# Two fused layers on one core: the last head pair's attention output is turned by a DMA transpose instead of TensorE

## The chip, the cores and the metric

The kernel runs on one core of one Trainium2 chip. The metric is the device time of one execution in microseconds (us). Engines are named as the profile names them: PE is TensorE (PEld its weight loads), DVE is VectorE, ACT is ScalarE, POOL is GpSimd, SP is SyncE, which here only issues DMAs.

## The reference, cut to what matters

Causal attention over 4 batches, 8 heads, 768 positions and head size 64, in which some heads see everything before them and the others only 4 sink positions and a window of 64. Its output, as 3072 tokens by 512, goes through a linear layer, a PReLU with one slope per column and a second linear layer:

```python
mask = np.where(retr[0, :, 0, 0, None, None], full_mask, stream_mask)
scores = np.where(mask[None, :, :, :], scores, -1000000000.0)
a = softmax(scores)                       # over the keys
attn_out = np.matmul(a, v)                # (4, 8, 768, 64)
x = attn_out.transpose(0, 2, 1, 3).reshape(B * S, H * D)
h = x @ w_in                              # 512 -> 2048
g = np.maximum(h, 0.0) + alpha * np.minimum(h, 0.0)
return (g @ w_out).astype(np.float32)     # 2048 -> 512
```

## The kernel before

The heads of a batch are taken two at a time, in the pairs (2, 6), (1, 5), (0, 4), (3, 7); with four batches that makes 16 pairs, numbered n = 0 to 15, so that pairs 12 to 15 are the last batch. Every piece of work is an item with a name, and the list `ORDER` gives the order in which all items are issued, written out by hand. Each engine runs its own share of that list in order; between engines, semaphores hold an instruction until its inputs are there. The items that matter here, with n a pair, h one of its two heads and m a part:

- `Sn.h.m` are the score matmuls (PE, L421 to L438), `sn.h.m` their exponentials on ACT (L477 for heads that see everything, L524 and L526 for windowed ones), and `mn.h.m` the masks, which DVE multiplies in (L486, and L535 with L538 for windowed heads).
- `An.h` is the product of the exponentials with the values on PE (L562), `an.h` the division by the row sums on DVE (a reciprocal, L572, and a product, L573) into a buffer `xn`.
- `Xn` turns `xn`, in which rows are tokens, into `xT`, in which columns are tokens. Pairs 0 to 3 do it in `X_pe`, with one transpose of TensorE per tile into a PSUM bank (L587), and `xn` with a small x (`x15` and the like, L592) copies the bank to `xT` on DVE. Later pairs do it in `X_dma` (L581), one DMA transpose from SP's queue. Pair 15 is the exception among the later ones: it takes `X_pe` and the copy `x15`.
- `Pt.f` is a block of the first linear layer for token block t (t = 0 to 7, two per batch: 512 tokens and 256). It takes one PSUM bank and adds up four terms, one for each pair of the batch, in the order of the pairs (L607); so it reads all four pairs' rows of `xT`, pair 15's last in batch 3. `pt.f` is the first half of the PReLU on ACT (L612), `gt.f` the second on DVE (L619).
- `Ot.s.u` is a quarter of an output piece of the second layer, four matmuls of 512 columns (L627); `ot.s` copies the finished piece out of its bank on ACT (L633) and writes it to memory (L637), from POOL's queue for t below 6 and from SP's above. `L0` to `L2` and `l0` to `l2` are the last piece, cut in three (L646, L655, L656).

Pair 15 is a pair of two windowed heads, with seven tiles of 112 queries each. A PSUM bank is taken by `take`, which picks the one given back longest ago, and is given back by `give`. So the order of the items also settles which bank each of them gets.

The buffer `xn` has three copies in use in turn; the fourth pair of a batch writes the copy that was used three pairs earlier and waits until the transfer that reads it is over.

In the last batch the items around the change are issued in this order: the products A12.1, A14.1 and A14.0, then six quarters of output pieces of blocks 4 and 5, then A15.0 and A15.1, two quarters, the seven transposes X15, one quarter, and then P6.11, the first block of the first layer for this batch. On SP's queue X13, X14 and X12 follow one another.

Of the kernel before, what the change touches and what calls it, by code (L numbers as in the profile page):

```python
# [63 lines left out]
m13.1.0 m14.0.0 m13.0.1 S14.0.5 S13.0.0 O4.2.2 O4.2.3 s13.1.2 m13.1.2 m13.1.1 s13.0.0 s14.0.4 s14.0.5 m13.0.2 S12.1.0 m12.1.5 s14.1.2 S12.1.3  # L64
S15.0.0 S14.0.3 m13.0.0 A13.1 o4.2 s12.1.0 s12.1.2 A13.0 s15.0.0 O5.0.0 s12.1.3 s14.0.3 m14.0.4 Cv15 a13.1 O5.0.1 a13.0 S15.0.1
S15.0.2 m12.1.0 S15.1.0 S15.1.2 S15.1.1 S14.0.2 O4.1.0 s15.0.2 s15.1.0 m12.1.4 s14.0.2 s15.1.1 m14.1.1 m14.0.5 m14.1.2 m12.1.3 m14.1.0 A12.1
m14.0.3 A14.1 A14.0 a14.0 s15.1.2 a14.1 m15.0.2 s15.0.1 a12.1 O4.1.1 X13 O4.0.0 O4.0.1 O4.0.2 O4.0.3 m15.0.0 m15.1.1 O4.1.2
m15.0.1 m15.1.2 m15.1.0 A15.0 o4.0 A15.1 a15.0 O4.1.3 a15.1 O5.0.2 X15 O5.0.3 X14 x15 o4.1 o5.0 X12 P6.11
p6.11 P6.2 P6.15 P6.10 p6.10 P7.4 P6.0 P6.1 g6.11 g6.10 p6.1 P6.6 P7.8 p6.15 g6.15 g6.1 p6.0 g6.0
P6.5 p7.4 p6.5 p6.6 g7.4 g6.6 g6.5 P6.3 P6.12 P7.2 p6.3 p6.12 g6.12 p6.2 g6.2 P6.4 p7.8 P7.6  # L70
P6.14 g6.3 g7.8 p7.6 p6.4 g7.6 g6.4 P7.10 P6.7 P6.8 p6.8 p6.7 P7.0 P6.9 P6.13 g6.7 p7.2 g7.2
g6.8 p7.10 g7.10 p6.9 P7.14 O6.3.0 P7.12 p6.13 g6.13 p7.12 O6.0.0 O6.0.1 O6.1.0 p7.0 g7.0 g6.9 O6.3.1 O7.0.0
O6.3.2 O6.1.1 p7.14 p6.14 g6.14 g7.12 O6.3.3 o6.3 O6.0.2 O6.1.2 O6.1.3 o6.1 O6.0.3 o6.0 O6.2.0 O6.2.1 O6.2.2 O7.0.1
O7.0.2 O6.2.3 o6.2 m12.0.2 g7.14 L2 l2 O7.0.3 o7.0 L0 L1 l1 warm1 l0
""".split()


# [1 line left out]
def kernel(  # L79
# [20 lines left out]
    bf16 = DT.bfloat16  # L100
# [4 lines left out]
    NT = 7  # L105
    SLOT = 288
    LAY = 4
# [24 lines left out]
    def tiles(n):  # L132
        return FULL if full(n) or mixed(n) else NEAR if n >= LAY else FAR
# [5 lines left out]
    NSEG = 4 * B  # L139
# [4 lines left out]
    work = ctx.enter_context(tc.tile_pool(name="work", bufs=2))  # L144
# [6 lines left out]
    def take(*choices):  # L151
        got = min((c for c in choices if all(age[b] >= 0 for b in c)), key=lambda c: max(age[b] for b in c))
        for b in got:
            age[b] = -1
        return got

    def give(got):
        for b in got:
            age[b] = stamp[0]
            stamp[0] += 1  # L160
# [3 lines left out]
    def bank(b):  # L164
        return P[:, b, :]

    def bank_bf(b):
        return P[:, b, :].bitcast(bf16)
# [34 lines left out]
    def heads(n):  # L203
        return PAIRS[n % 4]
# [89 lines left out]
    def item(name, fn, *args):  # L294
        I[name] = lambda: fn(*args)

    MISC = [(6,), (7,)]
    ANY = [(b,) for b in (0, 1, 2, 3, 4, 5, 6, 7)]
# [7 lines left out]
    natq, natk, held = {}, {}, {}  # L306
# [56 lines left out]
    def to_array(key, nat, choices, first_half=False):  # L363

        held[key] = take(*choices)
        tr = bank_bf(held[key][0])
        for i in range(6):
            if first_half:
                nc.tensor.transpose(tr[0:D, 128 * i:128 * (i + 1)], nat[:, i, 0:D], ident)
            else:  # L370
                nc.tensor.transpose(tr[:, 128 * i:128 * (i + 1)], nat[:, i, :], ident)
# [168 lines left out]
    xn = {}  # L540
# [24 lines left out]
    def AV_out(n, hh):  # L565
        got = held.pop(("A", n, hh))
        nt = len(tiles(n).QS)
        pav = bank(got[0])[:, 0:nt * (D + 1)].rearrange("p (i c) -> p i c", c=D + 1)
        if n not in xn:
            xn[n] = work.tile([128, NT, 128], bf16, tag="xn", name="xn", bufs=3)  # L570
        rcp = work.tile([128, NT, 1], fp32, tag=f"rcp{hh}", name="rcp")[:, 0:nt]
        nc.vector.reciprocal(rcp, pav[:, :, D:D + 1])  # L572
        nc.vector.tensor_tensor(xn[n][:, 0:nt, D * hh:D * hh + D], pav[:, :, 0:D],  # L573
                                rcp.to_broadcast([128, nt, D]), op=ALU.mult)
        give(got)
# [6 lines left out]
                          xn[n][0:r, 0:nt].rearrange("p i c -> p (i c)"), transpose=True)  # L582

    def X_pe(n):
        held["X", n] = got = take(*(MISC if n < 4 else ANY))
        for i, x in enumerate(tiles(n).QS):
            nc.tensor.transpose(bank_bf(got[0])[:, x:x + 128], xn[n][:, i, :], ident)  # L587

# [168 lines left out]
    for n in range(NSEG):  # L757
        if n:
            item(f"Lq{n}", load_q, n)
            item(f"Cq{n}", cast_q, n)  # L760
        item(f"Lk{n}", load_k, n)
        item(f"Lv{n}", load_v, n)
        if n == 3:
            for hh in range(2):
                item(f"Cv{n}.{hh}", cast_v_head, n, hh)
        else:
            item(f"Cv{n}", cast_v, n)
        if n < CROSS:
            for hh in range(2):
                item(f"Ck{n}.{hh}", cast_k, n, hh)  # L770
            if n:
                two = [(4,), (5,)] if n < 4 else ANY
                item(f"Tq{n}", lambda n=n, two=two: to_array(("q", n), natq[n], two))
                item(f"tq{n}", put_q, ("q", n), n, slice(0, 128), "A")
                item(f"Tk{n}", lambda n=n, two=two: to_array(("k", n), natk[n], two))
                for hh in range(2):
                    item(f"tk{n}.{hh}", put_k, ("k", n), n, hh, True)
        else:
            item(f"Ck{n}", cast_k_near, n)
            item(f"Dq{n}", dma_q, n)  # L780
            for hh in range(2):
                item(f"Dk{n}.{hh}", dma_k, n, hh)
        for hh, h in enumerate(heads(n)):
            k_ = (3 if n < 4 else 6) if RETR[h] else (2 if n < 4 else 3)
            for m in range(k_):
                item(f"S{n}.{hh}.{m}", S_retr if RETR[h] else S_stream, n, hh, m)
                item(f"s{n}.{hh}.{m}", E_retr if RETR[h] else E_stream, n, hh, m)
                if n >= 4:
                    item(f"m{n}.{hh}.{m}", M_retr if RETR[h] else M_stream, n, hh, m)
            item(f"A{n}.{hh}", AV, n, hh)  # L790
            item(f"a{n}.{hh}", AV_out, n, hh)
        if LAY <= n < NSEG - 1:
            item(f"X{n}", X_dma, n)
        else:
            item(f"X{n}", X_pe, n)
            item(f"x{n}", X_out, n)
# [61 lines left out]
```

## Time and profile before

| | |
|---|---|
| Median of 3 runs | 227.65 us (227.13 to 227.97) |
| Profiled execution, its own time | 227.53 us |
| Span of that execution in the profile | 225.8 us |
| PE busy | 221.3 us (98% of the span) |
| DVE busy, ACT busy, POOL busy | 148.4 (66%), 139.5 (62%), 45.2 (20%) us |
| PE's share of the chain that ended last | 70%; DMA 13%, SP's queue 11%, POOL 3% |
| Granted clock of TensorE | 1.0 |

The span is shorter than the execution's own time, by 1.7 us that lie around what the profiler sees. The chain that ended last is followed back from the last instruction: at each step to what released it. In the first 65 us it goes through loads and their issue on SP's queue, after that through PE. In a timeline a row gives the start in us, the length in us, the engine, the line, the operation and its operands; a bracket at its end tells how long the engine had been idle before it and what ended that. Matmuls are pipelined, so a single one looks longer in a timeline than the step from one to the next.

### The profile page before, as it was taken

How to read it: one execution, taken by the hardware profiler on the slowest of the kernel's cores; microseconds unless marked ns; L12 is line 12 of the kernel's file. 1: busy time of each engine (PE TensorE's matmuls, PEld its weight loads, DVE VectorE, ACT ScalarE, POOL GpSimd, SP SyncE). 2: the span in 40 equal slices, each digit the busy share in tenths (PEclk: the TensorE clock that was granted, in tenths of full speed). 3: DMA queues.
4: the chain of work that ended last, by engine and by line, in shares of the span. 5: the costliest groups of instructions: out<-in, count | busy, mean ns of one | idle time of the engine just before them, and what ended most of it. 6: DMA issues, size and time to landing. Idle time of an engine off the chain costs nothing.

```text
span 225.8 us, 5221 instructions
## 1 busy us (share of the span) xinstructions
PE 221.3 (98%) x1993; PEld 136.4 (60%) x1993; DVE 148.4 (66%) x396; ACT 139.5 (62%) x286; POOL 45.2 (20%) x91
## 2 busy tenths in 40 slices
PE   7999999999999999999999999999999999999994
PEld 7989876575555557564556455556556555664454
DVE  5799638995659618898798229977586526866000
ACT  3788668999888037577993147787584237563311
POOL 5689569400230001000401001000110100000000
DMA  6999999999999999999989999995822420000213
GB/s 200 310 242 207 266 214 273 212 196 218 198 245 222 140 245 190 197 190 186 236 194 153 237 231 205 188 164 108 124 94 40 115 96 0 0 4 0 93 71 116
DMA packets 95369, 37.38 MB, mean 166 GB/s; under 512 B 82392, under 2 KB 93552, under 8 KB 95344
## 3 DMA queue, kind: packets, MB, share of 16 engines
q1 hardware_dynamic: 89088, 27.72, 66.6%
q0 software_dynamic: 5792, 8.93, 17.1%
q10 hardware_dynamic: 464, 0.40, 0.5%
q8 instruction: 15, 0.25, 0.5%
q14 instruction: 10, 0.08, 0.1%
HBM read 27.71 MB, written 6.29 MB: 151 GB/s over the span
## 4 chain that ended last, share of the span: by engine, by line
PE 70%; DMA 13%; SPq 11%; POOL 3%; issue 1%; ACTq 0%; DVE 0%; POOLq 0%; DVEq 0%
PE P L627 31%; PE P L607 28%; DMA kf<-in_k_dram 8%; SPq L249 5%; PE P L562 5%; PE P L438 3%; DMA qf<-in_q_dram 3%; SPq L253 2%; DMA vf<-in_v_dram 2%; SPq L230 2%; PE P L646 2%; SPq L246 1%; POOL vb L356 1%; POOL g L322 1%; PE P L431 1%
## 5 line engine op out<-in xcount | busy, mean ns | idle before, releaser
L619 DVE SCALAR_TENSOR_TENSOR g<-neg,oma,P 128x256 bf16<-128x256 f32 (+1 forms) x128 | 71.0, 609 | 35.9 <-ACT neg L612 35.2
L607 PE MATMUL P<-xT,w_in_b 128*128 128x512 bf16 (+1 forms) x512 | 86.6, 326 | 0.0
L627 PE MATMUL P<-w_out_b,g 128*128 128x512 bf16 x368 | 85.3, 379 | 0.0
L612 ACT ACTIVATE neg<-P 128x512 f32<-128x512 f32 x96 | 54.2, 600 | 26.3 <-PE P L607 20.8
L607 PEld LDWEIGHTS <-w_in_b 128*128 128x128 bf16 x512 | 49.5, 98 | 32.3 <-DVE g L619 0.2
L627 PEld LDWEIGHTS <-g 128*128 128x128 bf16 x368 | 33.9, 98 | 37.2 <-issue 0.9
L477 ACT ACTIVATE eR<-P 128x448 bf16<-128x448 f32 (+3 forms) x63 | 35.9, 614 | 5.4 <-PE P L438 2.5
L633 ACT COPY ot<-P 128x512 f32<-128x512 f32 x23 | 13.8, 600 | 37.3 <-PE P L627 32.6
L637 POOL DMA_DIRECT2D out_dram<-ot x18 | 10.3, 574 | 108.9 <-ACT ot L633 108.7
L524 ACT ACTIVATE eS<-P 128x352 bf16<-128x352 f32 x45 | 20.4, 479 | 3.9 <-PE P L438 3.4
L573 DVE TENSOR_TENSOR xn<-P,rcp 128x448 bf16<-128x448 f32 (+1 forms) x32 | 19.0, 595 | 1.1
L535 DVE TENSOR_TENSOR eS<-eS,ms_near 128x352 bf16<-128x352 bf16 x45 | 14.4, 335 | 0.7 <-ACT eS L524 0.6
L572 DVE RECIPROCAL rcp<-P 128x7 f32<-128x7 f32 (+1 forms) x32 | 6.3, 197 | 11.2 <-PE P L562 10.5
L486 DVE TENSOR_TENSOR eR<-eR,mr_near 128x128 bf16<-128x128 bf16 x54 | 10.3, 219 | 3.9 <-ACT eR L477 3.7
L421 PE MATMUL P<-qT,kT 128*128 128x192 bf16 (+14 forms) x68 | 11.2, 251 | 0.2 <-DVE kT L394 0.2
L562 PEld LDWEIGHTS <-eS 128*128 128x128 bf16 x266 | 9.7, 97 | 2.3 <-issue 0.6
L562 PE MATMUL P<-vb,eS 128*128 128x65 bf16 x266 | 10.8, 193 | 0.0
L438 PEld LDWEIGHTS <-kT 64*128 64x128 bf16 x167 | 6.7, 94 | 6.1 <-issue 5.5
L438 PE MATMUL P<-qT,kT 64*128 64x176 bf16 (+7 forms) x167 | 10.3, 250 | 0.0
L562 PE MATMUL P<-vb,eR 128*128 128x65 bf16 x258 | 9.9, 193 | 0.1
L562 PEld LDWEIGHTS <-eR 128*128 128x128 bf16 x258 | 9.1, 97 | 1.4 <-issue 0.2
L655 DVE COPY ot<-P 128x128 f32<-128x128 f32 x1 | 0.3, 292 | 14.3 <-PE P L646 14.3
(96 smaller groups left out, 176.9 us busy)
## 6 DMA issues: line engine op xcount, KB each, us to landing
out_dram<-ot POOLq DMA_DIRECT2D x18, 256.0 KB, 3.9
kf<-in_k_dram SPq DMA_DIRECT2D x21, 192.0 KB
qf<-in_q_dram SPq DMA_DIRECT2D x18, 192.0 KB
vf<-in_v_dram SPq DMA_DIRECT2D x14, 196.0 KB
qf<-in_q_dram SPq DMA_DIRECT2D x7, 384.0 KB
vf<-in_v_dram SPq DMA_DIRECT2D x12, 192.0 KB
w_in_b<-in_moe_w_in_dram POOLq DMA_DIRECT2D x8, 256.0 KB, 9.1
w_out_b<-in_moe_w_out_dram POOLq DMA_DIRECT2D x4, 512.0 KB, 13.7
```

Of the source, the lines that this page charges most:

```text
L249: (nc.gpsimd if n == 13 and src is k else nc.sync).dma_start(dst[0:NSINK, :, hh, :], dram(src, o, [[D, NSINK], [0, NT], [1, D]]))
L438: nc.tensor.matmul(to, keys[own], queries[own], start=True, stop=True)
L477: nc.scalar.activation(ebuf[n, hh][:, lo:hi].rearrange("p (x c) -> p x c", x=len(parts)), P[:, got[0]:got[0] + len(parts), 0:(hi - lo) // ...
L524: nc.scalar.activation(slots, sc[:, 0:352].rearrange("p (s c) -> p s c", c=176), AF.Exp, scale=scale)
L535: nc.vector.tensor_tensor(slots, slots, ms_near[:, 0:2, :] if m == 0 else ms_near[:, 1:3, :], op=ALU.mult)
L562: nc.tensor.matmul(pav[:, i, :], e[:, o:o + 128], vv[:, j, hh, 0:D + 1], start=(m == 0), stop=(m == len(terms) - 1))
L573: nc.vector.tensor_tensor(xn[n][:, 0:nt, D * hh:D * hh + D], pav[:, :, 0:D], rcp.to_broadcast([128, nt, D]), op=ALU.mult)
L607: nc.tensor.matmul(psg[:, w * i:w * (i + 1)], w_in_b[:, c, 128 * fb:128 * (fb + 1)], xT[:, c, o:o + w], start=(x == 0), stop=(x == 3))
L612: nc.scalar.activation(neg[t, f], bank(held["P", t, f][0]), AF.Relu, scale=-1.0)
L619: nc.vector.scalar_tensor_tensor(g_buf[t % 2][:, fb, 0:w], neg[t, f][:, c], oma[:, fb:fb + 1], bank(got[0])[:, c], op0=ALU.mult, op1=ALU.add)
L627: nc.tensor.matmul(bank(held["O", t, s][0]), g_buf[t % 2][:, f, 128 * s:128 * (s + 1)], w_out_b[:, f, :], start=(f == 0), stop=(f == 15))
L633: nc.scalar.copy(ot, bank(got[0]))
```

## The change

Pair 15's output is turned by `X_dma`, one more DMA transpose on SP's queue, in place of seven transposes on PE and the copy on DVE. In the order, the masks of pair 15 move up in front of the divisions a14 and a12.1, and the products A15.0 and A15.1 move up in front of eight output quarters that had stood partly before, partly after them. The output quarters keep their order; X14 and X12 are issued among them and X15 behind the last of block 4. The buffer `xn` gets four copies. The exception in `X_pe` for late pairs, which no pair uses any longer, goes. What stands before and after the three lines of `ORDER` below is the same (the lines behind are only broken differently).

```diff
 ORDER
-m14.0.3 A14.1 A14.0 a14.0 s15.1.2 a14.1 m15.0.2 s15.0.1 a12.1 O4.1.1 X13 O4.0.0 O4.0.1 O4.0.2 O4.0.3 m15.0.0 m15.1.1 O4.1.2
-m15.0.1 m15.1.2 m15.1.0 A15.0 o4.0 A15.1 a15.0 O4.1.3 a15.1 O5.0.2 X15 O5.0.3 X14 x15 o4.1 o5.0 X12 P6.11
+m14.0.3 A14.1 A14.0 s15.1.2 m15.0.0 m15.0.2 m15.1.0 s15.0.1 m15.1.1 O4.1.1 X13 m15.1.2 m15.0.1 a14.0 a14.1 A15.0 A15.1 a12.1
+O4.0.0 X14 O4.0.1 O4.0.2 O4.0.3 X12 o4.0 a15.0 O4.1.2 a15.1 O4.1.3 X15 o4.1 O5.0.2 O5.0.3 o5.0 P6.11
...
     def AV_out(n, hh):
...
-            xn[n] = work.tile([128, NT, 128], bf16, tag="xn", name="xn", bufs=3)
+            xn[n] = work.tile([128, NT, 128], bf16, tag="xn", name="xn", bufs=4)
...
     def X_pe(n):
-        held["X", n] = got = take(*(MISC if n < 4 else ANY))
+        held["X", n] = got = take(*MISC)
...
-        if LAY <= n < NSEG - 1:
+        if n >= LAY:
             item(f"X{n}", X_dma, n)
         else:
             item(f"X{n}", X_pe, n)
             item(f"x{n}", X_out, n)
```

More of the change, by code (lines that the diff above doesn't have):

```diff
@@ L66 @@
 S15.0.2 m12.1.0 S15.1.0 S15.1.2 S15.1.1 S14.0.2 O4.1.0 s15.0.2 s15.1.0 m12.1.4 s14.0.2 s15.1.1 m14.1.1 m14.0.5 m14.1.2 m12.1.3 m14.1.0 A12.1
-m14.0.3 A14.1 A14.0 a14.0 s15.1.2 a14.1 m15.0.2 s15.0.1 a12.1 O4.1.1 X13 O4.0.0 O4.0.1 O4.0.2 O4.0.3 m15.0.0 m15.1.1 O4.1.2
-m15.0.1 m15.1.2 m15.1.0 A15.0 o4.0 A15.1 a15.0 O4.1.3 a15.1 O5.0.2 X15 O5.0.3 X14 x15 o4.1 o5.0 X12 P6.11
[L69 to L74, printed above, removed]
+m14.0.3 A14.1 A14.0 s15.1.2 m15.0.0 m15.0.2 m15.1.0 s15.0.1 m15.1.1 O4.1.1 X13 m15.1.2 m15.0.1 a14.0 a14.1 A15.0 A15.1 a12.1
+O4.0.0 X14 O4.0.1 O4.0.2 O4.0.3 X12 o4.0 a15.0 O4.1.2 a15.1 O4.1.3 X15 o4.1 O5.0.2 O5.0.3 o5.0 P6.11 p6.11
+P6.2 P6.15 P6.10 p6.10 P7.4 P6.0 P6.1 g6.11 g6.10 p6.1 P6.6 P7.8 p6.15 g6.15 g6.1 p6.0 g6.0 P6.5
+p7.4 p6.5 p6.6 g7.4 g6.6 g6.5 P6.3 P6.12 P7.2 p6.3 p6.12 g6.12 p6.2 g6.2 P6.4 p7.8 P7.6 P6.14
+g6.3 g7.8 p7.6 p6.4 g7.6 g6.4 P7.10 P6.7 P6.8 p6.8 p6.7 P7.0 P6.9 P6.13 g6.7 p7.2 g7.2 g6.8
+p7.10 g7.10 p6.9 P7.14 O6.3.0 P7.12 p6.13 g6.13 p7.12 O6.0.0 O6.0.1 O6.1.0 p7.0 g7.0 g6.9 O6.3.1 O7.0.0 O6.3.2
+O6.1.1 p7.14 p6.14 g6.14 g7.12 O6.3.3 o6.3 O6.0.2 O6.1.2 O6.1.3 o6.1 O6.0.3 o6.0 O6.2.0 O6.2.1 O6.2.2 O7.0.1 O7.0.2
+O6.2.3 o6.2 m12.0.2 g7.14 L2 l2 O7.0.3 o7.0 L0 L1 l1 warm1 l0
 """.split()
```

## The prediction

> **What bounds the kernel now.** I read the page's busy table first, then the chain that ended last in the stretch which the change touches, then the DVE, ACT and SP timelines there, and last the DMA shares by stage. TensorE (PE) is busy for 98% of the span:
>
> ```profile
> PE 221.3 (98%) x1993; PEld 136.4 (60%) x1993; DVE 148.4 (66%) x396; ACT 139.5 (62%) x286; POOL 45.2 (20%) x91
> ```
>
> The chain of waits from 170 to 186 us (start, length, what) runs on PE alone, with no step on another engine:
>
> ```profile
> 170.41 1.73 PE P L562 x57
> 172.14 5.18 PE P L627 x24
> 177.32 0.79 PE P L562 x26
> 178.11 1.73 PE P L627 x8
> 179.83 0.39 PE P L587 x7
> 180.22 0.86 PE P L627 x4
> 181.09 4.97 PE P L607 x27
> ```
>
> The reader sees in it the order of the code: A12.1, A14.1, A14.0 (L562), six output pieces of four matmuls (L627), A15.0 and A15.1, two pieces, the seven transposes X15 (L587), one piece, and then P6.11 (L607). PE never waits here, so an instruction that is taken off PE is worth its own time, and everything else is worth something only if it makes PE wait. From 181.09 to 222.70 the chain stays on PE (L607, L627, L646); the start of that block carries over to the end one to one.
>
> **The change part by part.** (1) Seven transposes leave PE: the chain gives 0.39 us for them, 56 ns each; the four matmuls after them take 0.86 us and the eight before 1.73, 0.216 each, so the switch costs nothing besides. Worth -0.39 us, and this is on the path. (2) The copy x15 (L592, 0.56 us) leaves DVE. DVE starts it at 180.26 and its next work, a prelu at 182.62, waits for ACT: worth nothing. (3) The masks m15 and the products A15 move up. What their masks need is this, in the DVE and the ACT timeline:
>
> ```profile
> 169.89 0.22 DVE L486 TENSOR_TENSOR eR<-eR,mr_near 128x128 bf16<-128x128 bf16 x1
> 172.25 0.20 DVE L572 RECIPROCAL rcp<-P 128x6 f32<-128x6 f32 x1 [2.13 <-PE P L562]
> ...
> 174.71 1.09 DVE L535 TENSOR_TENSOR eS<-eS,ms_near 128x352 bf16<-128x352 bf16 x4
> 175.72 0.20 DVE L538 TENSOR_TENSOR eS<-eS,ms_near 128x96 bf16<-128x96 bf16 x1
> 175.84 0.33 DVE L535 TENSOR_TENSOR eS<-eS,ms_near 128x352 bf16<-128x352 bf16 x1
> ```
>
> ```profile
> 171.24 0.31 ACT L526 ACTIVATE eS<-P 128x96 bf16<-128x96 f32 x1
> 171.37 0.53 ACT L524 ACTIVATE eS<-P 128x352 bf16<-128x352 f32 x1
> ```
>
> DVE is idle for 2.13 us after m14.0.3, waiting for A14.0. All eight mask instructions of pair 15 now stand in that hole: six of 0.26 us and two of 0.12 (steps from start to start) are 1.8 us of work. The first five can run from 170.02 on as their exponentials come; m15.1.2 needs the ACT instruction that ends at 171.55, and the last, m15.0.1, the one that ends at 171.90. So m15.0.1 runs from 171.94 to 172.28, and the reciprocal of a14.0 starts at about 172.25, where it starts now. Cost on DVE: nothing, hidden by the 2.13 us; without that cover it would be the 1.8 us, given on to a14, a12 and the transfers. On PE, A15.0 now comes after one output piece: 172.14 + 0.86 = 173.00. Its weight load that needs the last mask comes at about 172.9, so that mask has 0.6 us to spare. If it were later than that, PE and all that is queued on it would wait, one to one.
>
> (4) On DVE then a14.0, a14.1, a12.1 (0.70 us apart as now) end by 174.44, and a15.0, a15.1 (0.78 each, as in the rows from 177.75 to 179.38 now) by 175.98: A15.1 has ended on PE at 173.00 + 0.79 = 173.79, so they don't wait for it. The wait that a15.0 had for the landing of X13 goes with the fourth buffer; it had been over long before (X13's packets end at 171.0) and costs nothing now, so its loss is worth nothing. (5) One transfer is added on SP's queue, X15, behind X13, X14 and X12. X14 goes at 173.76 and X12 at 175.06 as now, because SP is held by X14 until 174.97 in both. X12 holds SP for 1.24 us, so X15 starts on SP at 176.36. Behind it on SP are only the outputs of blocks 6 and 7, from 201 on: nobody waits for that. The output writes of blocks 4 and 5 go through POOL; o4.0 now comes after PE's 173.79 + 3.46 = 177.25 and its write moves past X15's packets.
>
> When must X15 have landed? PE goes from 173.79 through 32 output matmuls, 32 x 0.216 = 6.91, to 180.70. P6.11 starts there, and its fourth matmul, the one that reads pair 15's rows of xT, is at 180.70 + 3 x 0.216 = 181.35. That is 5.0 us after X15 started on SP. The page gives no landing time for these transposes, so I bound it. From above by X7, the same pair's transfer two batches earlier (seven tiles of 112 rows too), in the SP timeline and the chain of that stage:
>
> ```profile
> 77.72 1.22 SPq L581 DMA_TRANSPOSE xT<-xn  x1
> ```
>
> ```profile
> 74.55 6.04 PE P L627 x28
> 80.60 17.34 PE P L607 x108
> ```
>
> There, too, the fourth matmul of the first block reads it, at 80.60 + 0.65 = 81.25, and PE did not wait: it landed within 3.53 us, while loads of later pairs shared the DMA engines. From below by X13 (seven tiles of 112 rows like X15), started on SP at 168.46; in the DMA shares (last two columns: share of the engines, GB/s) its packets are these:
>
> ```profile
> 169.60:170.00 0.40, 0.40 (x3) 0.19 (x2) 0.40 (x3) 0.40 (x3) 0.00 (x0) 1.00 0.78 152
> 170.00:170.40 0.40, 0.40 (x7) 0.24 (x6) 0.11 (x1) 0.40 (x2) 0.00 (x0) 1.00 1.10 208
> 170.40:170.80 0.40, 0.40 (x20) 0.40 (x17) 0.00 (x0) 0.40 (x2) 0.00 (x0) 1.00 0.70 142
> ```
>
> They end 2.4 us after the start. Between 2.4 and 3.5 us, X15 lands between 178.8 and 179.9 and has 1.5 to 2.5 us to spare. I take the upper end; both ends cost nothing. It is a close cover and not a wide one: 1.5 us later than X7's bound and PE begins to wait.
>
> The Trainium skill (VectorE: DVE Perf Modes, "The three transpose paths" and "Rules for kernel authors") speaks against this change: it gives 390 ns for one 128x128 turn on TensorE and 1309 ns by DMA, and advises TensorE where the result may go to PSUM. By its price the seven turns would be 2.73 us of PE; the trace has 0.39 us for all seven, queued back to back, and the trace decides.
>
> (6) P6 and P7 take other banks. The list of takes and gives is the same with the bank numbers exchanged, and each bank is given back before its next block needs it (the latest, o5.0's, serves P6.6, seven blocks on). Worth nothing.
>
> Sum against the profiled execution: span 225.80 - 0.39 = 225.41, and with the 1.73 us that lie around it (227.53 - 225.80) 227.14. That execution is 0.12 below the median of the three runs; on the median the forecast is 227.65 - 0.39 = 227.26.
>
> **The rivals.** *X15 lands late (slower).* Mechanism: the seven tiles are turned one after another, each as slow as a whole issue on SP, 1.22 us. Then it lands at 176.36 + 8.54 = 184.90 and PE waits 3.55 us in front of P6.11's fourth matmul: +3.16, 230.8. It begins to cost when the landing takes over 5.0 us, and gives a slower kernel by over 1.14 us (0.5%) from 6.5 us on. Against it: X7's 3.53 us and X13's packets, both of seven tiles. Taken one after another, the Trainium skill's 1309 ns a tile (VectorE: DVE Perf Modes, "The three transpose paths") would lead to the same wait; no row here bears it out. Chance 0.04; a smaller wait that leaves the kernel within 0.5% gets 0.05, with a time up to 228.4.
>
> *The masks become the bound.* If m15.0.1 comes as late as it does now, 176.17, A15.0 waits 3.3 us: +2.9, 230.5. It decides from 172.9 on. For it: DVE runs in order, and one late exponential holds everything behind it. Against it: the last exponential is there at 171.90 and ACT's order does not change. Chance 0.01.
>
> *The gain is larger.* If the fourth buffer took away waits of DVE in other batches that PE pays for, or if the interruption of the output pieces cost more than its 0.39 us, the kernel would gain over 1.14 us, say 226.2. The waits of the matmul queue list none after 66 us, so there is hardly anything to take. Chance 0.02.
>
> *Nothing changes:* the 0.39 us are lost again at P6's start, 227.65. Possible if DVE set the pace of block 6 from its first prelu; but it waits for ACT there, 1.80 us before the first one. Chance 0.08; this leaves 0.80 for the forecast.
>
> **How the numbers follow.** 0.5% (1.14 us) is about what a measurement of this kernel can tell from no change. Faster by more: 0.02. Slower by more: 0.04 + 0.01 = 0.05. Within it: 0.93, from the forecast, the small wait and no change. The range takes the forecast with the scatter of the three runs (0.52 below and 0.32 above their median), and no change with a little of a wait: 226.75 to 227.85.
>
> **What would show it.** Right: no L587 after 170 us; A15.0 at about 173.0 with no idle time before it; 32 matmuls of L627 in one piece for 6.9 us; the last transpose starts on SP near 176.4; P6.11 at 180.7 and the span near 225.4. Wrong: idle time of PE in front of L607 at 181 (X15 late) or of L562 at 173 (masks late), a reciprocal of a14.0 well after 172.3, or a stretch after P6.11 that has become longer than 41.6 us.

## The result and the profile after

The changed kernel took 227.1 us (median of 22 runs), the kernel before, run beside it, 228.11 us (22 runs); disturbed runs are left out of the ratio, which is 0.9953 with a 95% interval of 0.9933 to 0.9973. The forecast was 227.26 us and 0.9983. The profiled execution of the changed kernel took 226.85 us with a span of 225.1 us, 0.7 less than the 225.8 before; the steps of the trace account for 0.39 + 0.18 of it, and 0.11 stood there before the change begins.

PE's busy share is unchanged within what missing matmul records leave open (1958 records for 1986 weight loads here). The weight loads are seven fewer than before (1993), one for each transpose, and DVE has one instruction less, the copy:

```profile
PE 219.3 (97%) x1958; PEld 136.0 (60%) x1986; DVE 148.0 (66%) x395; ACT 139.5 (62%) x286; POOL 45.3 (20%) x91
```

The chain of waits in the stretch of the change, to be laid beside that of before:

```profile
170.30 1.73 PE P L562 x57
172.03 0.05 issue
172.08 0.81 PE P L627 x3
172.89 0.79 PE P L562 x26
173.68 4.32 PE P L627 x20
177.99 0.05 issue
178.05 2.54 PE P L627 x11
180.58 1.51 PE P L607 x7
```

A12.1, A14.1, A14.0, one output quarter, A15.0 and A15.1 directly behind it, then eight output quarters in one piece and P6.11. L587 is gone. An "issue" of 0.05 us with one matmul too few behind it (3 for 4, 20 and 11 for 32) is a matmul whose record is missing: the times go on without a gap. From the first L562 to the first L607 it was 181.09 - 170.41 = 10.68 us and is 180.58 - 170.30 = 10.28 us: 0.40 less. In PE's timeline, on which the table below rests, the two matmuls start at these times, first before, then after (10.67 and 10.28 us apart):

```profile
170.25 0.80 PE L562 MATMUL P<-vb,eR 128*128 128x65 bf16 x21
180.92 1.24 PE L607 MATMUL P<-xT,w_in_b 128*128 128x512 bf16 x5
```

```profile
170.14 0.80 PE L562 MATMUL P<-vb,eR 128*128 128x65 bf16 x21
180.42 1.89 PE L607 MATMUL P<-xT,w_in_b 128*128 128x512 bf16 x8
```

What follows P6.11 has not changed: from its start to the last copy on DVE (L655) 41.69 us before (181.09 to 222.78) and 41.70 after (180.58 to 222.28).

DVE's timeline shows the masks in the hole that was 2.13 us of idle time before:

```profile
169.78 0.22 DVE L486 TENSOR_TENSOR eR<-eR,mr_near 128x128 bf16<-128x128 bf16 x1
169.92 0.59 DVE L535 TENSOR_TENSOR eS<-eS,ms_near 128x352 bf16<-128x352 bf16 x2
...
171.83 0.34 DVE L535 TENSOR_TENSOR eS<-eS,ms_near 128x352 bf16<-128x352 bf16 x1
172.09 0.19 DVE L572 RECIPROCAL rcp<-P 128x6 f32<-128x6 f32 x1
```

The last mask begins 1.69 us after A12.1 (170.14 in PE's timeline), and the reciprocal of a14.0 has no idle time in front of it. X15 goes out on SP's queue here, right after X12:

```profile
176.23 1.24 SPq L581 DMA_TRANSPOSE xT<-xn  x1
```

By the landing records of the trace it landed 2.80 us later, at 179.03; the fourth matmul of P6.11 starts at 181.07 in PE's timeline. It had 2.0 us to spare.

The other 0.18 us lie at the very end. The last copy on DVE, first before, then after:

```profile
222.78 0.29 DVE L655 COPY ot<-P 128x128 f32<-128x128 f32 x1 [14.31 <-PE P L646]
```

```profile
222.28 0.29 DVE L655 COPY ot<-P 128x128 f32<-128x128 f32 x1 [14.31 <-PE P L646]
```

From its start to the end of the span it was 3.05 us before and is 2.87 after (the spans, unrounded, are 225.82 and 225.15 us). The waits of SP's queue at the kernel's end, first before, then after (total, times, longest):

```profile
SPq L853 <- DMA out_dram<-ot: 0.8, 1, 0.8
```

```profile
SPq L853 <- DMA out_dram<-ot: 0.3, 1, 0.3
```

At its end SP goes through all semaphores of transfers in one fixed list of waits. The transfers that SP and ACT issue take their semaphores in turn from one ring. With one transfer more on SP's queue every later one uses the next semaphore (the last write has number 108 instead of 107), so the last write's wait stands one place later in the list: two waits follow it in the kernel before, one in the changed kernel. By the records of the traces, 0.23 us pass from that landing to the end of the list before and 0.15 after. The last write itself lands 1.65 us after its start before and 1.56 after; why those 0.09 us go with the semaphore is not settled. The ten traces of this document fall into two groups by these figures, five without the additional transfer and five with it.

### The profile page after: what moved, and what is told of

Same layout as the page of the kernel before. It is cut to its first block, busy times and chain, and to the rows that moved or that the text cites. A ratio compares the mean times of both kernels' runs of the same rounds, so it can differ in the third digit from the quotient of the medians.

```text
span 225.1 us, 5178 instructions
## 1 busy us (share of the span) xinstructions
PE 219.3 (97%) x1958; PEld 136.0 (60%) x1986; DVE 148.0 (66%) x395; ACT 139.5 (62%) x286; POOL 45.3 (20%) x91
## 4 chain that ended last, share of the span: by engine, by line
PE 84%; SPq 9%; DMA 2%; issue 2%; ACT 1%; DVE 0%; POOL 0%; DVEq 0%; POOLq 0%; ACTq 0%
PE P L627 31%; PE P L607 31%; PE P L562 7%; SPq L249 6%; PE P L438 3%; PE P L421 3%; PE P L698 3%; DMA vf<-in_v_dram 2%; SPq L253 2%; PE P L646 2%; SPq L246 2%; PE P L371 1%; PE P L508 1%; PE P L587 1%; PE P L431 1%
## 5 line engine op out<-in xcount | busy, mean ns | idle before, releaser
L607 PE MATMUL P<-xT,w_in_b 128*128 128x256 bf16 (+1 forms) x501 | 85.7, 325 | 0.6
L627 PE MATMUL P<-w_out_b,g 128*128 128x512 bf16 x351 | 83.0, 379 | 1.0 <-issue 0.2
L607 PEld LDWEIGHTS <-w_in_b 128*128 128x128 bf16 x512 | 49.5, 98 | 32.3 <-DVE g L619 0.2
L562 PEld LDWEIGHTS <-eS 128*128 128x128 bf16 x266 | 9.7, 97 | 2.3 <-issue 0.6
L562 PE MATMUL P<-vb,eS 128*128 128x65 bf16 x266 | 10.8, 193 | 0.0
L562 PE MATMUL P<-vb,eR 128*128 128x65 bf16 x258 | 9.9, 193 | 0.1
L562 PEld LDWEIGHTS <-eR 128*128 128x128 bf16 x258 | 9.1, 97 | 1.4 <-issue 0.2
L655 DVE COPY ot<-P 128x128 f32<-128x128 f32 x1 | 0.3, 292 | 14.3 <-PE P L646 14.3
```

The lines of the kernel that those rows point to most:

```text
L562: nc.tensor.matmul(pav[:, i, :], e[:, o:o + 128], vv[:, j, hh, 0:D + 1], start=(m == 0), stop=(m == len(terms) - 1))
L607: nc.tensor.matmul(psg[:, w * i:w * (i + 1)], w_in_b[:, c, 128 * fb:128 * (fb + 1)], xT[:, c, o:o + w], start=(x == 0), stop=(x == 3))
L627: nc.tensor.matmul(bank(held["O", t, s][0]), g_buf[t % 2][:, f, 128 * s:128 * (s + 1)], w_out_b[:, f, :], start=(f == 0), stop=(f == 15))
```

## The experiments

Each has a profile; the stretch from the first matmul of A12.1 to the first of P6.11 and the one from the last copy to the end of the span are read from PE's and DVE's timelines. The page rounds spans to 0.1 us; the fourth column uses them unrounded.

| kernel | A12.1 starts | to P6.11 | last copy to end | ratio to before (95% interval) |
|---|---|---|---|---|
| before | 170.25 | 10.67 | 3.05 | |
| changed | 170.14 | 10.28 | 2.87 | 0.9953 (0.9933 to 0.9973) |
| before, again | 170.33 | 10.67 | 3.05 | 0.9995 (0.9966 to 1.0024) |
| changed, again | 169.91 | 10.28 | 2.87 | 0.9961 (0.9933 to 0.9989) |
| fourth buffer alone | 169.95 | 10.67 | 3.04 | 0.9994 (0.9969 to 1.0019) |
| change with three buffers | 169.69 | 10.28 | 2.86 | 0.9980 (0.9953 to 1.0007) |
| moved, turned by PE | 171.48 | 10.67 | 3.04 | 1.0016 (0.9998 to 1.0034) |
| by DMA, not moved | 170.03 | 10.28, its fourth matmul 1.59 late | 2.86 | 1.0042 (1.0026 to 1.0057) |
| turned twice by PE | 170.18 | 11.06 | 3.04 | 1.0018 (0.9986 to 1.0050) |
| masks behind the divisions | 174.14 | 15.0 | 2.87 | 1.0193 (1.0167 to 1.0220) |

The instructions up to A12.1 are the same in all ten, but for the waits that the fourth buffer removes. Still its start scatters, by 0.6 us among the first six and by 1.8 among the first nine, and this makes the intervals wide. Nearly all of it arises in the loading phase: counted back from A12.1, PE's earlier groups of L562 stand at the same distances, to 0.02 us, from about 71 us on in eight of the ten traces; in the fourth buffer alone and the masks behind the divisions 0.29 and 0.19 us more were lost near 113 us.

**The two kernels once more.** No edit. Theory A was that only the seven transposes count, theory B that something else, the fourth buffer above all, gives the rest of the measured 0.47%.

> The kernel before once more, against itself, as a measure of what the comparison can tell. Theory A (only PE's 0.39 us were gained, the rest of the measured 0.47% is scatter of the first 65 us and of the end): a ratio of 1.000, with an interval that is about 0.002 wide to each side. Theory B (the fourth buffer or something else gives 0.3% more): also 1.000, but then the interval must be narrow enough to tell 0.995 from 0.998. PE's block P6.11 starts near 181.1 us.

> The changed kernel once more. Theory A: the start of P6.11 lies 0.4 us behind the start of A12.1 less than in the kernel before (10.28 instead of 10.68 us), and the ratio is nearer to 0.998 than to 0.995. Theory B: the ratio stays at 0.995.

The middle came out at 10.67 and 10.28 us to the hundredth. The ratio of the kernel before to itself covers 1 with 0.003 to each side, wider than expected: a difference of 0.17% can't be read from times alone, and the stretches of the traces have to carry the argument. The changed kernel's second ratio, 0.9961, is nearer to B's 0.995 than to A's 0.998, and its interval holds both; the times alone don't decide here.

**The fourth buffer alone, and the change without it.**

```diff
-            xn[n] = work.tile([128, NT, 128], bf16, tag="xn", name="xn", bufs=3)
+            xn[n] = work.tile([128, NT, 128], bf16, tag="xn", name="xn", bufs=4)
```

> Only the fourth buffer. Theory A: nothing, ratio 1.000, and 10.68 us from A12.1 to P6.11 as before; the three waits of DVE that go with it had been over before DVE came to them. Theory B: 0.997, with the gain seen before 170 us.

> The whole change without the fourth buffer. Theory A: the same as the changed kernel, 10.28 us from A12.1 to P6.11, ratio 0.998. Theory B: the ratio comes back to within 0.002 of 1.

The fourth buffer alone: 0.9994, 10.67 us, the end as before. Without it: 10.28 us, the end as in the changed kernel, 0.9980. That ratio by itself fits both theories, which had 0.998 and "within 0.002 of 1"; the stretches decide. Theory B falls in the form that names the buffer: with the buffer alone neither stretch is shorter, and the whole change without it keeps both gains. What the buffer could give before A12.1 is bounded by the ratio of 0.9994 alone, to about 0.3%.

**The moves without the DMA.**

```diff
 changed kernel, ORDER
-O4.0.0 X14 O4.0.1 O4.0.2 O4.0.3 X12 o4.0 a15.0 O4.1.2 a15.1 O4.1.3 X15 o4.1 O5.0.2 O5.0.3 o5.0 P6.11
+O4.0.0 X14 O4.0.1 O4.0.2 O4.0.3 X12 o4.0 a15.0 O4.1.2 a15.1 O4.1.3 X15 o4.1 O5.0.2 x15 O5.0.3 o5.0 P6.11
...
-        if n >= LAY:
+        if LAY <= n < NSEG - 1:
             item(f"X{n}", X_dma, n)
```

(The exception in `X_pe` for late pairs comes back with this edit.)

> The order of the changed kernel and its four buffers, but pair 15 turned by seven transposes of PE and the copy on DVE. Theory A (the gain in the middle is the seven transposes alone): 10.67 us from the start of A12.1 to the start of P6.11, as in the kernel before; the moves are worth nothing by themselves. And since SP's queue has one transfer less, the last 256 columns' write uses the same semaphore as before, so that 3.03 us lie between the start of the last copy (L655 on DVE) and the end of the span, not 2.85. Theory B (the order gives the gain, because an interrupted run of output pieces costs PE something): 10.3 us.

The chain of this kernel has the transposes back and with them the time:

```profile
180.19 0.39 PE P L587 x7
180.59 1.73 PE P L627 x8
182.31 5.84 PE P L607 x31
```

10.67 us, and 3.04 us at the end, as theory A had it. The moves alone are worth nothing, and the gain at the end goes with the additional transfer on SP and not with the order.

**The DMA without the moves.**

```diff
 kernel before, ORDER
-O5.0.2 X15 O5.0.3 X14 x15 o4.1 o5.0 X12 P6.11
+O5.0.2 O5.0.3 X14 o4.1 o5.0 X12 X15 P6.11
...
-        if LAY <= n < NSEG - 1:
+        if n >= LAY:
             item(f"X{n}", X_dma, n)
```

> The kernel before with pair 15 turned by DMA, issued behind X12, and nothing moved; three buffers. Theory A (landing takes 2.80 us from the start on SP, as for X15 in the changed kernel): a15.1 ends 9.13 us after A12.1 starts, X15 starts 0.04 us later and lands 11.97 us after A12.1; the fourth matmul of P6.11 is due at 10.28 + 0.65 = 10.93, so PE waits 1.0 us in front of it, and the kernel is 0.65 us slower in the middle than before. The end has 2.85 us from the start of the last copy, as in the changed kernel. Rival (seven tiles turned one after another, 1.22 us each): it lands 8.5 us after its start, PE waits 6.8 us and the kernel is 6.4 us slower. Theory B (no transposes on PE is all that counts): 10.28 and no wait.

Its chain goes through the transfer, and PE's timeline shows the wait in front of P6.11's fourth matmul:

```profile
179.19 3.32 DMA xT<-xn
```

```profile
180.31 0.81 PE L607 MATMUL P<-xT,w_in_b 128*128 128x512 bf16 x3
182.55 3.62 PE L607 MATMUL P<-xT,w_in_b 128*128 128x512 bf16 x19 [1.43 <-DMA xT<-xn]
```

The bracket counts from the recorded end of the third matmul, which lasts longer than the step to the next one. By the steps of 0.216 us the fourth was due at 180.96 and started at 182.55, so PE lost 1.59 us, for 1.0 expected, because the landing took 3.32 us and not 2.80. The DMA shares of that time (last two columns: share, GB/s):

```profile
180.50:181.00 0.50, 0.50 (x3) 0.20 (x2) 0.00 (x0) 0.45 (x1) 0.00 (x0) 1.00 1.03 192
181.00:181.50 0.50, 0.12 (x1) 0.00 (x0) 0.00 (x0) 0.14 (x1) 0.07 (x1) 1.00 1.13 268
181.50:182.00 0.50, 0.00 (x0) 0.00 (x0) 0.00 (x0) 0.00 (x0) 0.47 (x1) 1.00 0.94 336
```

An output write that POOL issued at 179.71 falls into the same time. The packet records tell the two apart. X15's data packets (256 bytes each) run from 180.37 to 181.52, 1.15 us, and are hardly slower than those of X13 in the kernel before (169.63 to 170.77). The output write's packets of 4 KB start at 181.31. What comes late is the 4-byte packets that end X15's transfer: for X13 they were over with the last data, at 170.78, here they run among the write's packets until 182.18. By these records it is the end of the transfer that the write held up. In the changed kernel the two do not meet, since o4.0's write starts at 179.20, behind X15's last packet at 178.60. The time adds up: -0.39 + 1.59 - 0.18 = +1.02 us, 1.0045; measured 1.0042. The rival with seven tiles one after another (a wait of 6.8 us) is refuted, and so is theory B.

**The masks behind the divisions.** The masks of pair 15 go behind a14.0, a14.1 and a12.1 on DVE; PE's order stays that of the changed kernel.

```diff
 changed kernel, ORDER
-s15.1.2 m15.0.0 m15.0.2 m15.1.0 s15.0.1 m15.1.1 O4.1.1 X13 m15.1.2 m15.0.1 a14.0 a14.1 A15.0 A15.1 a12.1
+s15.1.2 s15.0.1 O4.1.1 X13 a14.0 a14.1 a12.1 m15.0.0 m15.0.2 m15.1.0 m15.1.1 m15.1.2 m15.0.1 A15.0 A15.1
```

> The changed kernel with pair 15's masks behind a14.0, a14.1 and a12.1 on DVE instead of in front of them. Theory A (the hole of 2.1 us on DVE hides the masks): the three divisions end at about 4.2 us after A12.1 starts and the last mask at 6.0; PE is ready for it at 2.6, so PE waits 3.3 us in front of A15.0 and P6.11 starts at 13.5 instead of 10.28; the ratio to the kernel before is 1.012. X15 still lands before P6.11 needs it. Rival (the masks' place does not matter, DVE has time to spare): 10.28.

PE's timeline has two waits for masks, 2.93 us together by their brackets. Counted, as above, from when the next matmul was due, they are 3.3 us, as expected:

```profile
178.62 0.30 PE L562 MATMUL P<-vb,eS 128*128 128x65 bf16 x4 [1.73 <-DVE eS L535]
180.11 1.39 PE L562 MATMUL P<-vb,eS 128*128 128x65 bf16 x22 [1.20 <-DVE eS L535]
```

But the stretch took 15.0 us and not 13.5. The rest is the clock; in the table by stage its granted share is the third column from the right:

```profile
180.00:182.00 2.00, 1.89 (x24) 1.49 (x25) 1.16 (x5) 0.00 (x0) 0.00 (x0) 0.50 0.50 98
182.00:184.00 2.00, 2.00 (x8) 0.78 (x7) 0.45 (x1) 0.00 (x0) 0.00 (x0) 0.70 0.15 28
184.00:186.00 2.00, 2.00 (x11) 0.94 (x10) 0.00 (x0) 0.06 (x1) 0.00 (x0) 1.00 0.37 72
```

Behind the waits PE ran at half its clock for 3.4 us (179.80 to 183.22 in the clock's records), and matmuls of 512 columns went 0.43 us apart instead of 0.216. PE worked through the last 3.1 us of that, from 180.11 on, and lost half of them: 1.55 us. All five executions of this kernel have a mean granted clock of 0.985 to 0.993, those of the four other kernels run beside it 0.998 to 1.0, so the fall belongs to the kernel. This execution's loading phase was about 4 us longer than in the others (A12.1 starts at 174.14), which does not touch the stretch. The place of the masks in the hole is what the whole change stands on: without it, the kernel is 1.9% slower than before (1.2% expected, without the clock).

**Seven transposes more.**

```diff
+    def X_again(n):
+        for i, x in enumerate(tiles(n).QS):
+            nc.tensor.transpose(bank_bf(held["X", n][0])[:, x:x + 128], xn[n][:, i, :], ident)
...
 kernel before, ORDER
-O5.0.2 X15 O5.0.3 X14 x15
+O5.0.2 X15 Y15 O5.0.3 X14 x15
```

> The kernel before with the seven transposes of pair 15 made twice, into the same bank. Theory A (seven transposes cost PE 0.39 us when queued back to back): 11.06 us from A12.1 to P6.11, 0.39 more than before. Rival (each transpose costs PE as much as 390 ns, which the Trainium skill gives for one, VectorE: DVE Perf Modes, The three transpose paths): 2.7 us more, 13.4.

In its chain (lines are shifted by four; L591 is the second seven):

```profile
179.76 0.39 PE P L587 x7
180.15 0.39 PE P L591 x7
180.54 0.86 PE P L631 x4
```

11.06 us: the price of the first term is confirmed, 56 ns a transpose. The rival of 2.7 us is refuted.

## Why the prediction was right, point by point

- *Seven transposes leave PE, 0.39 us.* Right, to the hundredth: 10.67 us in four traces with the transposes, 10.28 in four without, and +0.39 when they were doubled. The Trainium skill's 390 ns for each (VectorE: DVE Perf Modes, "The three transpose paths") is not what seven of them cost in a queue that never empties, and its advice to turn on TensorE would have kept the slower kernel here.
- *The copy x15 and the fourth buffer, nothing.* Right for the buffer by an experiment; for the copy by the stretch after P6.11, which has the same length with it (the kernel before, the one moved but turned by PE) and without.
- *The masks fit into DVE's hole.* Right: the last one was to start 1.69 us after A12.1 (171.94 - 170.25) and did (171.83 - 170.14). The cover was priced too low: for masks as late as before the prediction had +2.9 us against the kernel before, and the experiment lost 4.3 us against it in the middle (15.0 for 10.67), since the prediction left out the clock.
- *X15 starts on SP at 176.36 and lands after 2.4 to 3.5 us.* It started 6.09 us after A12.1 (6.11 predicted) and landed in 2.80. The bound from X7 that I took, 3.53, was 0.7 too high; it cost nothing, as said. The landing records of the trace before, which the prediction did not use, have 2.89 us for X7 and 2.81 for X13, but 4.8 to 5.9 for the three transfers of this kind from 66 to 76 us, where the DMA engines are busy over 90% of the time: a bound from one transfer holds only where the engines are as idle as there. The slack was 4.84 us (176.23 to 181.07) and not 5.0, because the prediction took PE's times from the chain, in which the same matmul stands 0.16 us later than in the timeline (170.41 and 170.25 for A12.1's first), and X15's start from the timeline. The margin of 2.0 us is within the 1.5 to 2.5 predicted.
- *The time of P6 and P7.* Unchanged, 41.7 us; the banks play no part.
- *What was missing.* The end of the kernel. The sum took the time from P6.11 to the end of the span as carried over one to one. It is so up to the last copy; the 0.18 us behind it, about half from the place of the last write's semaphore in the list of waits and half from its shorter landing, were in no step. So the gain that the traces show is 0.57 us, 0.9975, for 0.39 forecast. That the forecast of 227.26 us lies so near the measured 227.1 is partly luck: it started from 227.65, and the kernel before took 228.11 beside the changed one.
- *What stays open.* 0.9975 lies just outside the first interval (to 0.9973) and inside those of the other two comparisons. No row of the traces shows a further gain: up to A12.1 only the waits for the fourth buffer differ, and alone it gave 0.9994; from the group of L562 at about 71 us to A12.1 PE takes 99.23 us in both kernels. I take the rest for scatter of the loading phase; that it is nothing but scatter has not been shown.

## What to carry to other kernels

Where an engine's chain has no waits, taking an instruction off it is worth its step in the queue and not its latency: read it from the time from one start to the next, as 7 in 0.39 us, and not from the 219 ns that one of them shows. The price of the DMA in its place is all in the slack: make the inputs early, find the idle time that hides the work moved up (here 2.1 us on DVE for 1.8 us of masks), and count from the transfer's start to its first reader. When waits of some 3 us on TensorE are a rival, add what its clock loses afterwards (1.55 us here).

## What the runs showed of the hardware that was not expected

- A transposing transfer of six or seven tiles from SBUF to SBUF landed 2.73 to 2.83 us after its start on SP in the last batch, where the DMA engines were quiet (X13, X14, X12 and X15 in the changed kernel: 2.83, 2.73, 2.79, 2.80), in 3.32 when an output write's packets came between its data and the 4-byte packets that end it, and in 4.7 to 5.9 us for the three between 66 and 76 us in the kernel before and the changed one, where the DMA engines are busy over 90% of the time.
- Two waits of PE, 1.73 and 1.20 us with four small matmuls in between, were enough for the granted clock to fall to 0.5 for 3.4 us; one wait of 1.43 us was not (matmuls went on 0.216 us apart). The Trainium skill (TensorE: Matmul & The Clock Gate, "What's actually happening") puts the fall after an idle window of about 3.4 us. By its bracket the first wait began at 176.89 (178.62 - 1.73), 2.9 us before the fall at 179.80, so trace and page agree only roughly, and only if those four matmuls do not count as work.
- The last semaphore waits of the kernel follow each other 0.06 to 0.08 us apart once the last transfer has landed, so one place in that list is worth about as much as one transpose in PE's queue.
